# One more batch in folded form: batch 1's mirrored half goes through DRAM, and its first stage starts at unit 14

## The chip, the cores and the metric

The kernel runs on one core of one Trainium2 chip. The metric is the device time of one execution in microseconds (us). A profiled execution has a span, the time between its first and its last recorded instruction, and a device time a little longer than that. The engines are named as in the profile: PE is TensorE (matmuls) and PEld its weight loads, DVE is VectorE, ACT is ScalarE, POOL is GpSimd, SP is SyncE, which here only issues transfers.

## The reference

The input x has 8 batches of 3072 rows and 256 columns. The reference takes a Fourier transform along the rows and one along the columns, keeps the real part, and sends each of the 24576 rows through a layer with a maximum over three products:

```python
X = np.fft.fft(x, axis=1)
X = np.fft.fft(X, axis=2)
y = X.real.astype(np.float32).reshape(B * S, D)
h = np.maximum(np.maximum(y @ w1, y @ w2), y @ w3)
return (h @ w_out).astype(np.float32)
```

w1, w2, w3 are 256 x 768 and w_out is 768 x 256.

## The kernel before

**Work and units.** For each batch the transform is made in two matmul stages into a buffer `t` (`tE`, `tO`), and the layer runs on `t` in three blocks of 512 tokens with six column groups each: 18 units per batch (`UNITS`), 8 batches. By symmetry a unit makes two results at once, for the tokens and for their mirror images (`hp` and `hm`). A unit is `unit_plus` (four matmuls of 512 columns, L591 and L592), `unit_out` (a Relu on ACT, L605, a maximum on DVE, L606), `finish` of the unit before (two matmuls, L599, and again L605 and L606), and eight to ten matmuls of the output layer of the block before (L616). Beside them run `l2_even` (a product in PSUM, copied by ACT into `even`) and `l2_odd` (a product, DVE's `other` from it, L643, and POOL's `even` addition, L646). DVE adds them to the output (L670); one half of an output tile is stored by SP (L689), the other scattered by POOL (L677).

**Who runs when.** The order on each engine is the order in which the code writes instructions; there is no scheduler. The dictionary `plan` says which side work is written behind which unit: `at(b, unit, fn)` puts `fn` behind unit `unit` counted from the start of batch `b`, so unit 18 of batch 0 is unit 0 of batch 1. Each engine takes its instructions in that order, and one that waits holds all behind it. SP and POOL likewise issue their transfers in order.

**The transform of the next batch.** While batch b's units run, the transform of batch b + 1 is made (`ahead`, `begin`): seven parts s0 to s6 of stage one (`Mix.s`, L547), then six parts k0 to k5 of stage two (`Mix.k`, L571 and L573). Part s0 takes the rows d = 2 to 6 of the laid-out input, s1 7 to 11, and so on to s5 with 27 to 31; s6 takes 0, 32 and 1. A part writes one PSUM buffer of the pool `ps_f`, which has two, and ACT copies it out (L552, L555, L556; for stage two L575). Unit 0 of the next batch needs k0 and k1, unit 6 needs k2 and k3.

**The layout of the input.** Stage one needs batch b's rows in natural and in mirrored order. SP fetches a batch in four chunks of some 0.8 MB in f32 (`load_chunk`, L111 and L123) into four buffers `xs`; a chunk's buffer is used again for the next batch once all copies out of it are done.
- Batch 0 is laid out by ACT and DVE at the start and is not part of this.
- Batch 1 is unfolded. POOL copies each chunk in natural order (`turn_chunk`, L158) and in mirrored order (`reverse`, L160) into one buffer `x0`, for the last chunk in pieces (`turn_last`, L218 and L220, with `lay_last` on ACT, L209). Stage one takes two matmuls for each d, with the weights of the one and the other and the matrices `m24f` and `m24r`.
- Batches 2 to 7 are folded. `turn_part(b, ch, part)` copies a chunk on POOL: parts 0 and 1 write halves of its mirrored rows into `xb` (L178), part 1 also one row of `xw` (L182), parts 2 and 3 write halves of its natural rows into `xw` (L173). When all four chunks' mirrored halves are there, `send_turned` has SP write `xb` to DRAM in eight transfers of 96 KB with the order of partitions turned (`held`, L191). `add_turned(b, c)` then has POOL issue a transfer that reads a quarter of `held` back and adds it to `xw` in place (L199): c = 0 the rows d = 1 to 8, c = 1 9 to 16, c = 2 17 to 24, c = 3 25 to 32. After that each d takes one matmul, and only d = 0 takes two. There is one `xb`, and there are two `xw`.

For b = 0, 1 and later, the tuple `mirrored, natural, send_at, add_at` gives the units (counted from batch b) for the copies, sends and transfers of batch b + 2.

Of the kernel before, what the change touches and what calls it, by code (L numbers as in the profile page):

```python
# [33 lines left out]
def kernel(  # L34
# [9 lines left out]
    nc = tc.nc  # L44
# [101 lines left out]
                                 [xs.ap[0], [1, hi - lo], [-64, m]]))  # L146
        return done

    def turn_chunk(b, ch):

        if (b, "v") not in turned:
            x0 = x0_pool.tile([96, 68 * 128], BF16, name="x0", tag="x0")
            v = x0[:, 0:66 * 130].rearrange("p (dl bb) -> p dl bb", bb=130)
            turned[b] = (lambda d: v[:, d, 0:128], rows_back(v[:, 33:66, :]))
            turned[b, "v"] = v
        v = turned[b, "v"]
        xs = raw[b, ch]
        nc.gpsimd.tensor_copy(v[:, 0:33, ch * 32:ch * 32 + 32],  # L158
                              xs[:, 0:32 * 64].rearrange("p (bb dl) -> p dl bb", dl=64)[:, 0:33, :])
        reverse(lambda out, in_: nc.gpsimd.tensor_copy(out, in_), v[:, 33:66, :], xs,  # L160
                ch * 32, 33 if ch == 3 else 32)

    def turn_part(b, ch, part):

        xs = raw[b, ch]
# [39 lines left out]
        nc.scalar.activation(out=gw[:, 514:770], in_=gw[:, 256:512], func=AX.Copy, scale=sgn)  # L205

    def lay_last(part):
        d0, d1 = ((0, 8), (8, 16))[part]
        nc.scalar.copy(out=turned[1, "v"][:, d0:d1, 96:128],  # L209
                       in_=raw[1, 3][:, 0:32 * 64].rearrange("p (bb dl) -> p dl bb", dl=64)[:, d0:d1, :])  # L210

    def turn_last(half):

        v = turned[1, "v"]
        xs = raw[1, 3]
        d0, d1 = ((0, 17), (17, 33))[half]
        if half:
            nc.gpsimd.tensor_copy(v[:, 16:33, 96:128],  # L218
                                  xs[:, 0:32 * 64].rearrange("p (bb dl) -> p dl bb", dl=64)[:, 16:33, :])
        reverse(lambda out, in_: nc.gpsimd.tensor_copy(out, in_), v[:, 33:66, :], xs, 96, 33,  # L220
                32 + d0, 32 + d1)

    def rows_back(v):
        return lambda d: v[:, 32 - d, 0:128] if d else v[:, 32, 1:129]
# [617 lines left out]
    def fetch(b, ch):  # L842
# [1 line left out]

    ahead = (("s0",), ("s1",), ("s2",), ("s3",), ("s4",), ("s5",), ("s6",),
             ("k0",), ("k1",), ("k2",), ("k3",), ("k4",), ("k5", "end"))
    begin = {0: (11, 12, 13, 13, 14, 14, 15, 16, 16, 17, 18, 19, 20),
             1: (11, 12, 12, 13, 13, 14, 14, 15, 16, 17, 18, 19, 20),
             2: (10, 11, 11, 12, 12, 13, 13, 14, 15, 16, 17, 18, 19),
             B - 2: (8, 8, 9, 9, 10, 11, 11, 12, 13, 14, 15, 16, 17)}  # L850
# [7 lines left out]
    for (u, fn) in ((0, prep_some), (0, prep_some), (0, lambda: tab_sines(7, 10, (2,))),  # L858
                    (1, prep_some), (1, prep_some), (1, prep_some),
                    (2, lambda: m.k(2)), (2, prep_some), (2, lambda: tab_sines(10, 13, (0,))),  # L860
                    (3, prep_some), (3, lambda: tab_sines(10, 13, (1, 2))),
                    (4, lambda: m.k(3)), (4, prep_some), (5, prep_some), (5, l2_first),
                    (6, lambda: m.k(4)), (7, lambda: m.k(5)), (7, m.end),
                    (0, lambda: turn_chunk(1, 0)), (2, lambda: tab_minus(10, 13, nc.gpsimd)),
                    (2, lambda: turn_chunk(1, 1)),
                    (5, lambda: turn_chunk(1, 2)),
                    (7, lambda: turn_last(0)), (8, lambda: turn_last(1)),
                    (8, lambda: lay_last(0)), (9, lambda: lay_last(1)), (20, signed)):
        at(0, u, fn)
    for ch in range(4):  # L870
        at(0, (6, 7, 9, 11)[ch], lambda ch=ch: fetch(2, ch))
    for b in range(B - 1):
        for i, whats in enumerate(ahead):
            for what in whats:
                at(b, begin.get(b, steady)[i], lambda b=b, what=what: piece(b + 1, what))
        if b + 2 < B:
            mirrored, natural, send_at, add_at = (
                ((11, 11, 12, 13, 14, 15, 16, 17), (12, 13, 15, 16, 18, 18, 19, 20), 18, 22),
                ((5, 6, 9, 10, 11, 12, 13, 14), (7, 8, 12, 14, 15, 16, 17, 18), 15, 19),
                ((4, 5, 6, 7, 8, 9, 10, 11), (8, 10, 12, 13, 14, 15, 16, 17), 12, 18))[min(b, 2)]  # L880
            for i in range(8):
# [89 lines left out]
```

## Time and profile before

| | |
|---|---|
| median of 3 runs | 404.83 us (404.59 to 404.92) |
| the profiled execution | 404.64 us, span 402.9 us |
| PE busy | 386.0 us, 96% of the span |
| POOL busy | 292.0 us, 72% |
| DVE busy | 308.9 us, 77% |
| ACT busy | 265.5 us, 66% |
| moved by DMA | 62.06 MB, 154 GB/s |

The page gives busy times and shares per engine, then groups of instructions: line, engine, operation, output<-input, shape, count, then busy time and the mean of one in ns, then the idle time of the engine before them and what ended it. A timeline row is the start in us from the span's beginning, the time in us, and the instruction with its count; where a stretch holds several of the same kind, it runs from the first to the last. On SP and POOL the time of a transfer's row is that of issuing it, not of its data. The DMA rows of a window give the packets that moved in it, by size, and the share per queue: q1 is SP's queue, q0 that of POOL. A matmul's own duration is that of a pipeline, longer than the distance from one to the next.

### The profile page before, as it was taken

Reading aid. Unit: us, or ns where it says so; the run is one execution under the profiler, and the core shown is the slowest. Engines: PE = TensorE matmul, PEld = TensorE weight load, DVE = VectorE, ACT = ScalarE, POOL = GpSimd, SP = SyncE. Lnnn points to the kernel's source line nnn. Section 1 sums busy time; section 2 is a strip of 40 time slices with the busy share of each in tenths; the row PEclk is TensorE's granted clock in tenths of the full one; section 3 lists DMA queues with packets and bytes.
Section 4 is the critical chain, followed back from the end, with each engine's and each line's share of the span. In section 5 each row is a group of like instructions: output and inputs, shape, how many; then the busy total and the mean of one; then the engine's idle time right before and its main releaser. Section 6 shows DMA issues by size and latency. Waiting matters only on the chain.

```text
span 402.9 us, 8560 instructions
## 1 busy us (share of the span) xinstructions
PE 386.0 (96%) x2829; PEld 260.6 (65%) x2877; DVE 308.9 (77%) x556; ACT 265.5 (66%) x489; POOL 292.0 (72%) x394
## 2 busy tenths in 40 slices
PE   0999999999999999999999999999999999999996
PEld 0465667666676667666666666666677676666665
DVE  8898776788777877687776887787777877678884
ACT  6787767655866667756766677666766676655550
POOL 9599889879986998679877888768967524323521
PEclk9999999999999999999999999999999999999999
DMA  9989897789778838875478928886234411211214
GB/s 117 188 199 179 157 226 197 174 213 196 186 197 214 192 120 217 193 184 159 114 200 186 227 78 222 197 191 179 81 103 114 123 55 74 84 52 54 103 57 156
DMA packets 127597, 62.06 MB, mean 154 GB/s; under 512 B 111616, under 2 KB 116736, under 8 KB 126976
## 3 DMA queue, kind: packets, MB, share of 16 engines
q1 hardware_dynamic: 101976, 42.21, 42.3%
q0 software_dynamic: 24640, 18.98, 23.8%
q8 instruction: 22, 0.36, 0.4%
q10 hardware_dynamic: 936, 0.33, 0.3%
q14 instruction: 23, 0.19, 0.2%
HBM read 33.74 MB, written 29.88 MB: 158 GB/s over the span
## 4 chain that ended last, share of the span: by engine, by line
PE 85%; DVE 4%; DMA 3%; POOL 2%; ACT 2%; issue 2%; DVEq 0%; SPq 0%; POOLq 0%; ACTq 0%
PE po L616 29%; PE pse L591 16%; PE pse L599 14%; PE pse L592 12%; PE ps L571 3%; PE ps L573 3%; PE po L640 3%; PE pl L629 2%; PE ps L547 2%; POOL x L111 2%; DMA raw_w<-in_moe_w_dram 2%; DVE hm L606 2%; ACT stmp L605 2%; DMA x<-in_x_dram 2%; DVE other L643 1%
## 5 line engine op out<-in xcount | busy, mean ns | idle before, releaser
L605 ACT ACTIVATE stmp<-pse 128x512 bf16<-128x512 f32 x288 | 170.8, 600 | 52.6 <-PE pse L592 26.2
L606 DVE TENSOR_TENSOR hp<-pse,stmp 128x512 bf16<-128x512 f32 x144 | 99.5, 691 | 80.1 <-ACT stmp L605 51.8
L646 POOL TENSOR_TENSOR even<-even,other 128x256 f32<-128x256 f32 x92 | 70.1, 762 | 74.5 <-DVE other L643 74.2
L591 PE MATMUL pse<-t,gE 128*128 128x512 bf16 x288 | 109.1, 379 | 2.5
L606 DVE TENSOR_TENSOR hm<-pse,stmp 128x512 bf16<-128x512 f32 x144 | 99.2, 689 | 3.3 <-ACT stmp L605 3.1
L592 PE MATMUL pse<-t,gO 128*128 128x512 bf16 x249 | 94.3, 379 | 0.0
L616 PE MATMUL po<-wout_bf,hp 128*128 128x256 bf16 x576 | 85.9, 272 | 0.0
L616 PE MATMUL po<-wout_bf,hm 128*128 128x256 bf16 x570 | 85.3, 273 | 0.3
L599 PE MATMUL pse<-t,gD 128*128 128x512 bf16 x279 | 83.7, 379 | 0.1
L677 POOL DMA_INDIRECT out_dram<-ot,rows_m x53 | 53.8, 1015 | 20.2 <-DVE ot L670 10.7
L616 PEld LDWEIGHTS <-hp 128*128 128x128 bf16 x576 | 56.3, 98 | 17.3 <-issue 2.5
L616 PEld LDWEIGHTS <-hm 128*128 128x128 bf16 x576 | 56.4, 98 | 16.5
L670 DVE TENSOR_TENSOR ot<-po,even 128x512 f32<-128x512 f32 x92 | 62.8, 682 | 0.0
L173 POOL CAST xw<-xs 96x544 bf16<-96x544 f32 (+1 forms) x48 | 53.2, 1120 | 0.0
L178 POOL CAST xb<-xs 96x512 bf16<-96x512 f32 x48 | 52.4, 1100 | 0.0
L575 ACT CAST t<-ps 128x512 bf16<-128x512 f32 x48 | 27.9, 585 | 34.8 <-PE ps L573 34.7
L599 PEld LDWEIGHTS <-gD 128*128 128x128 bf16 x288 | 28.1, 98 | 32.2
L643 DVE SCALAR_TENSOR_TENSOR other<-twice,po 128x256 f32<-128x256 f32 x92 | 43.8, 476 | 0.1
L592 PEld LDWEIGHTS <-gO 128*128 128x128 bf16 x288 | 28.1, 98 | 20.4 <-issue 1.9
L591 PEld LDWEIGHTS <-gE 128*128 128x128 bf16 x288 | 28.2, 98 | 19.5 <-issue 0.7
L552 ACT CAST z_all<-ps 128x480 bf16<-128x480 f32 x46 | 24.8, 560 | 22.0 <-PE ps L547 21.9
L632 ACT COPY even<-pl 128x512 f32<-128x512 f32 x46 | 27.0, 587 | 9.7 <-PE pl L629 8.6
(178 smaller groups left out, 370.9 us busy)
## 6 DMA issues: line engine op xcount, KB each, us to landing
xs<-in_x_dram SPq DMA_DIRECT2D x84, 198.0 KB
out_dram<-ot SPq DMA_DIRECT2D x39, 256.0 KB
xs<-in_x_dram SPq DMA_DIRECT2D x28, 192.0 KB
held<-xb SPq DMA_DIRECT2D x48, 96.0 KB
xw<-held POOLq DMA_DIRECT2D x24, 192.0 KB
raw_w<-in_moe_w_dram SPq DMA_DIRECT2D x4, 384.0 KB
out_dram<-ot SPq DMA_DIRECT2D x12, 128.0 KB
x<-in_x_dram POOLq DMA_DIRECT2D x8, 120.0 KB
```

The source lines that it names most:

```text
L173: nc.gpsimd.tensor_copy(v[:, d0:d1, ch * 32:ch * 32 + 32], xs[:, 0:32 * 64].rearrange("p (bb dl) -> p dl bb", dl=64)[:, d0:d1, :])
L178: nc.gpsimd.tensor_copy(mir[:, d0:d1, c0:c0 + 32], bass.AP(xs.tensor, xs.offset + 33 * 64 - 1 - d0, [xs.ap[0], [-1, d1 - d0], [-64, 32]]))
L591: nc.tensor.matmul(pse[:, 0:n], gE[i][:, js], te, start=True, stop=False)
L592: nc.tensor.matmul(pse[:, 0:n], gO[i][:, js], to, start=False, stop=True)
L599: nc.tensor.matmul(pse, gD[i][:, js], to, start=False, stop=True, skip_group_check=True)
L605: nc.scalar.activation(out=stmp[:, 0:n], in_=pses[0][:, 0:n], func=AX.Relu)
L606: nc.vector.tensor_tensor(out=dst, in0=src3, in1=stmp[:, 0:n], op=ALU.max)
L616: nc.tensor.matmul(po, hcols(jc), wout_bf[:, jc * 256:(jc + 1) * 256], start=False, stop=(jc == NJC - 1), skip_group_check=True)
L643: nc.vector.scalar_tensor_tensor(out=other, in0=twice, scalar=po[:, 256:257], in1=po[:, 0:256], op0=ALU.mult, op1=ALU.subtract)
L646: nc.gpsimd.tensor_tensor(out=line[:, 256:512], in0=line[:, 0:256], in1=other, op=ALU.add)
L670: nc.vector.tensor_tensor(out=parts, in0=po.rearrange("p (i c) -> p i c", i=2), in1=lin.rearrange("p (i c) -> p i c", i=2), op=ALU.add)
L677: stored(nc.gpsimd.indirect_dma_start(out.rearrange("(n two) c -> n (two c)", two=2) if pair else out, bass.IndirectOffsetOnAxis(ap=rows_m ...
```

## The change

Batch 1 takes the folded form. `turn_chunk` and `turn_last` are gone. POOL makes batch 1's layout with 15 calls of `turn_part`, behind units 0 to 10 of batch 0, and ACT's `lay_last` makes the sixteenth piece (now 17 rows d in two steps, where it was 16). The eight sends stand behind unit 8, the four accumulating transfers behind units 12, 12, 13 and 13. Stage one of batch 1 stands behind units 14 to 16 in place of 11 to 15, and stage two one unit later than before, k0 and k1 both behind unit 17. Stage one of batch 1 has 32 matmuls less (34 in place of 66).

The copies of batch 2 stand one to three units later, its sends at unit 20 in place of 18, its transfers from unit 24 in place of 22; a few copies of batch 3 stand one unit later. Batch 2's third and fourth fetch stand one unit later, batch 3's first three one or two units later.

In the order of SP, batch 1's eight sends stand behind batch 2's first two chunks and one store. In the order of POOL, the four transfers stand together, ahead of batch 2's first copy and of the `even` addition of unit 14.

```diff
-    def turn_chunk(b, ch):
...
     def lay_last(part):
-        d0, d1 = ((0, 8), (8, 16))[part]
-        nc.scalar.copy(out=turned[1, "v"][:, d0:d1, 96:128],
+        d0, d1 = ((0, 8), (8, 17))[part]
+        nc.scalar.copy(out=turned[1][:, d0:d1, 96:128],
...
-    def turn_last(half):
...
-    begin = {0: (11, 12, 13, 13, 14, 14, 15, 16, 16, 17, 18, 19, 20),
+    begin = {0: (14, 14, 15, 15, 16, 16, 16, 17, 17, 18, 19, 20, 21),
...
-                    (0, lambda: turn_chunk(1, 0)), (2, lambda: tab_minus(10, 13, nc.gpsimd)),
-                    (2, lambda: turn_chunk(1, 1)),
-                    (5, lambda: turn_chunk(1, 2)),
-                    (7, lambda: turn_last(0)), (8, lambda: turn_last(1)),
+                    (2, lambda: tab_minus(10, 13, nc.gpsimd)),
                     (8, lambda: lay_last(0)), (9, lambda: lay_last(1)), (20, signed)):
         at(0, u, fn)
+    for (u, ch, part) in ((0, 0, 0), (0, 0, 1), (0, 0, 2), (0, 0, 3), (2, 1, 0), (2, 1, 1),
+                          (2, 1, 2), (4, 1, 3), (5, 2, 0), (5, 2, 1), (6, 2, 2), (7, 3, 0),
+                          (7, 3, 1), (9, 2, 3), (10, 3, 3)):
+        at(0, u, lambda ch=ch, part=part: turn_part(1, ch, part))
+    at(0, 8, lambda: send_turned(1))
+    for c in range(4):
+        at(0, 12 + c // 2, lambda c=c: add_turned(1, c))
     for ch in range(4):
-        at(0, (6, 7, 9, 11)[ch], lambda ch=ch: fetch(2, ch))
+        at(0, (6, 7, 10, 12)[ch], lambda ch=ch: fetch(2, ch))
...
             mirrored, natural, send_at, add_at = (
-                ((11, 11, 12, 13, 14, 15, 16, 17), (12, 13, 15, 16, 18, 18, 19, 20), 18, 22),
-                ((5, 6, 9, 10, 11, 12, 13, 14), (7, 8, 12, 14, 15, 16, 17, 18), 15, 19),
+                ((13, 14, 14, 15, 16, 17, 18, 19), (15, 16, 17, 18, 20, 21, 22, 23), 20, 24),
+                ((6, 7, 9, 10, 11, 12, 13, 14), (8, 9, 12, 14, 15, 16, 17, 18), 15, 19),
                 ((4, 5, 6, 7, 8, 9, 10, 11), (8, 10, 12, 13, 14, 15, 16, 17), 12, 18))[min(b, 2)]
...
-                    at(b, ((15, 18, 20, 26), (11, 15, 17, 23), (11, 14, 16, 22))[min(b, 2)][ch],
+                    at(b, ((17, 19, 22, 26), (11, 15, 17, 23), (11, 14, 16, 22))[min(b, 2)][ch],
```

More of the change, by code (lines that the diff above doesn't have):

```diff
@@ L147, in reverse @@
         return done
-    def turn_chunk(b, ch):
[L151 to L161, printed above, removed]
     def turn_part(b, ch, part):
@@ L207, in lay_last @@
     def lay_last(part):
-        d0, d1 = ((0, 8), (8, 16))[part]
-        nc.scalar.copy(out=turned[1, "v"][:, d0:d1, 96:128],
+        d0, d1 = ((0, 8), (8, 17))[part]
+        nc.scalar.copy(out=turned[1][:, d0:d1, 96:128],
                        in_=raw[1, 3][:, 0:32 * 64].rearrange("p (bb dl) -> p dl bb", dl=64)[:, d0:d1, :])
-    def turn_last(half):
[L214 to L221, printed above, removed]
     def rows_back(v):
```

## The prediction

> **What bounds the kernel now.** I read the page first, its busy shares and its chain.
>
> ```profile
> span 402.9 us, 8560 instructions
> PE 386.0 (96%) x2829; PEld 260.6 (65%) x2877; DVE 308.9 (77%) x556; ACT 265.5 (66%) x489; POOL 292.0 (72%) x394
> PE 85%; DVE 4%; DMA 3%; POOL 2%; ACT 2%; issue 2%; DVEq 0%; SPq 0%; POOLq 0%; ACTq 0%
> ```
>
> TensorE is busy for 96% of the span and is 85% of the chain. So a matmul taken away is time gained, and any time in which TensorE has to wait for its next operand is time lost; nothing later gives it back. The other engines matter only where they deliver something late. The change does both things: it takes matmuls away, and it gives one stage an operand with a longer way to go. So I read the timeline of TensorE at the place, batch 0's units 14 and 15 (columns: start, us, instruction, count).
>
> ```profile
> 58.49 0.21 PE L547 MATMUL ps<-m24f,x 96*128 96x96 bf16 x1
> ...
> 59.37 0.38 PE L591 MATMUL pse<-t,gE 128*128 128x512 bf16 x1
> ...
> 61.65 0.21 PE L547 MATMUL ps<-m24f,x 96*128 96x96 bf16 x1
> ...
> 62.50 0.81 PE L591 MATMUL pse<-t,gE 128*128 128x512 bf16 x2
> ```
>
> Unit 14 starts at 59.37, its own matmuls end at 61.65, then come two parts of stage one (20 matmuls), and unit 15 starts at 62.50. There is no gap anywhere. The 20 matmuls from 58.49 to 59.37 take 0.88 us, so one costs 0.044 us of TensorE, not the 0.2 us of its pipelined duration.
>
> **What is removed.** Unfolded, stage one of a batch has 66 matmuls (two for each of 33 rows d); folded it has 34 (row 0 has two). 32 fewer times 0.044 is 1.4 us. All of it is on the path. This is the whole possible gain.
>
> **When stage one now wants its data.** Before, four parts stood ahead of unit 14's end (after units 11, 12, 13, 13), 40 matmuls or 1.75 us. They move behind, so unit 14 ends at 61.65 - 1.75 = 59.9, and there TensorE stands before part s0, whose first weights (rows 2 to 6) lie in the piece that accumulating transfer 0 adds to. Part s1 (rows 7 to 11) needs transfer 1 as well.
>
> **When the data can be there.** It goes GpSimd copies, eight sends on SP, four accumulating transfers from GpSimd. First GpSimd, from its timeline and its groups:
>
> ```profile
> 30.52 2.04 POOL L158 CAST x<-xs 96x1056 bf16<-96x1056 f32 x1
> 46.05 1.17 POOL L220 CAST x<-xs 96x561 bf16<-96x561 f32 x1 [1.06 <-DMA xs<-in_x_dram]
> 53.83 0.72 POOL L646 TENSOR_TENSOR even<-even,other 128x256 f32<-128x256 f32 x1 [1.61 <-DVE other L643]
> L178 POOL CAST xb<-xs 96x512 bf16<-96x512 f32 x48 | 52.4, 1100 | 0.0
> L173 POOL CAST xw<-xs 96x544 bf16<-96x544 f32 x24 | 28.0, 1167 | 0.0
> L173 POOL CAST xw<-xs 96x512 bf16<-96x512 f32 x24 | 25.8, 1073 | 0.0
> L182 POOL CAST xw<-xs 96x32 bf16<-96x32 f32 x24 | 6.2, 259 | 0.0
> L199 POOL DMA_DIRECT2D xw<-held x24 | 26.8, 1178 | 0.6 <-POOL even L646 0.6
> L646 POOL TENSOR_TENSOR even<-even,other 128x256 f32<-128x256 f32 x92 | 70.1, 762 | 74.5 <-DVE other L643 74.2
> ```
>
> The first copy of batch 1 starts at 30.52. A chunk costs 2 x 1.10 + 0.26 + 1.17 + 1.07 = 4.7 us. Chunks 0 and 1 with a table operation of 1.2 us and one `even` (0.76) bring it to 41.9; chunk 2's mirrored copies, one `even` and a natural part to 46.3; chunk 3, which the second row shows landed at 46.05, is mirrored by 48.8. Behind it stand three `even`s, two scattered stores of about 1 us, two natural parts, and then a fourth `even`, that of unit 12, whose operand comes from DVE. The `even` of unit 11 ran at 53.83 after such a wait; unit 12 is 2.3 us later, so this one is done near 57. In all batch 1 now costs GpSimd 8 x 1.10 + 4 x 0.26 + 7 x 1.12 + 4 x 1.18 = 22.4 us where six copies of 2.04 and about 3.5 us for the last chunk were 15.7. These 6.7 us cost TensorE nothing by themselves, because the queue of SP is later still. SP's timeline:
>
> ```profile
> 40.88 3.03 SPq L123 DMA_DIRECT2D xs<-in_x_dram  x5
> 44.01 8.24 SPq L111 DMA_DIRECT2D xs<-in_x_dram  x8
> 52.34 1.22 SPq L689 DMA_DIRECT2D out_dram<-ot  x1
> 53.66 3.96 SPq L111 DMA_DIRECT2D xs<-in_x_dram  x4
> 74.68 4.12 SPq L191 DMA_DIRECT2D held<-xb  x8
> 199.81 4.77 SPq L191 DMA_DIRECT2D held<-xb  x8
> ```
>
> In the changed program's order the eight sends of batch 1 stand right behind batch 2's first two chunks (44.01, eight transfers) and one store (52.34). Nothing ahead of them moves, since chunk 3 of batch 1 holds SP until 43.9 either way. So the first send is issued at 53.6, five microseconds after its data was ready. How long the eight then take, from the DMA view in windows (the sends are the packets that are not under 8 KB):
>
> ```profile
> DMA packets 259, 0.88 MB, mean 147 GB/s; under 512 B 139, under 2 KB 139, under 8 KB 162
> DMA packets 2382, 1.75 MB, mean 208 GB/s; under 512 B 2126, under 2 KB 2126, under 8 KB 2286
> DMA packets 1861, 0.47 MB, mean 174 GB/s; under 512 B 1861, under 2 KB 1861, under 8 KB 1861
> q1 hardware_dynamic: 1516, 0.61, 98.3%
> ```
>
> The first row is 74.6 to 80.6: with little else about, all 96 packets have gone 5.9 us after the first issue at 74.68. The second is 199.8 to 208.2: behind a fetch the 96 took 8.4 us. The third is the first 2.7 us of that, in which five sends were issued and not one packet of theirs moved: 1861 small ones of the fetch went first. The fourth is 53.6 to 56.2 of this profile, just when the new sends will be issued: SP's queue alone keeps the engines 98.3% busy with batch 2. So it is the loaded case: 7.9 us, near the second row's end of 5.9 to 8.4, and the sends are through at 61.5 (59.5 to 62.0). GpSimd reached the first accumulating transfer at 57 and waits 4.5 us there. Queued behind that wait are the other three (1.18 us each), batch 2's copies, and the `even` of unit 14, which then runs at about 61.5 + 4.7 + 1.1 = 67.3 to 68.1; DVE's addition to the output waits for it, so this is what would be late next if the transfers were quick.
>
> What an accumulating transfer takes, from the GpSimd timeline and the DMA windows 305.8 to 307.5, 307.5 to 312.0 and 216.4 to 221.4:
>
> ```profile
> 213.39 2.07 POOL L199 DMA_DIRECT2D xw<-held  x2
> DMA packets 0, 0.00 MB, mean 0 GB/s; under 512 B 0, under 2 KB 0, under 8 KB 0
> xw<-held POOLq DMA_DIRECT2D x2, 192.0 KB
> q0 software_dynamic: 414, 0.39, 58.0%
> q0 software_dynamic: 368, 0.41, 52.2%
> ```
>
> After two are issued nothing at all moves for 1.7 us, on idle engines; then their 0.39 MB take 4.5 us. That is 6.2 us for two with nearly nothing beside them. The pair issued at 213.39 beside a fetch was through at 221.4, 8.0 us later. Batch 2's third and fourth chunk will run beside the new ones, so I take 7.7: transfers 0 and 1 are there at 61.5 + 7.7 = 69.2 (65.7 with both light ends, 70.0 with both loaded ends). Two units need transfers 2 and 3 later, and by then those are there too.
>
> **The sum.** Unit 15 starts at 69.2 in place of 62.50: +6.7 us, in which the removed matmuls of four parts are already counted. Then four folded parts follow that used to be ahead, 4 x 5 x 0.044 = +0.9, less 0.1 for the shorter part s6. Three parts now stand behind unit 16 and share two PSUM buffers, so s6 waits for the copy of s4; and k1, which used to follow unit 16, follows unit 17, with only two matmuls (0.43 us) between it and the unit that reads its copy:
>
> ```profile
> L552 ACT CAST z_all<-ps 128x480 bf16<-128x480 f32 x46 | 24.8, 560 | 22.0 <-PE ps L547 21.9
> L575 ACT CAST t<-ps 128x512 bf16<-128x512 f32 x48 | 27.9, 585 | 34.8 <-PE ps L573 34.7
> ```
>
> A copy of 0.56 less the 0.22 of s5, plus about 0.2 to get there: +0.5 (0 to 1). A copy of 0.585 and a matmul's 0.27 less 0.43: +0.4 (0 to 1). Last the clock. TensorE's own rows at the kernel's start, after 10 us of idling (windows, the `warm` matmuls alone):
>
> ```profile
> 10.00:13.90 3.90, 3.89 (x10) 1.00 2.65 124
> 13.90:16.20 2.30, 2.30 (x12) 1.00 1.88 133
> ```
>
> Ten matmuls of 512 columns fill the first 3.9 us, twelve the next 2.3: about half speed at first (the column of the granted clock says 1.00 in both, so the pace must be read from the counts). A wait of 69.2 - 59.9 = 9 us, broken by one short part, is nearest to these 10 us, so I count one such start: 3.9 us at half speed, +1.9 (0 to 3.9, if it is paid twice). The Trainium skill, "TensorE: Matmul & The Clock Gate", Part 1, has the clock halved after one idle window of about 3.4 us and restored after one busy window; by it the price is due even at the short end of my range of waits, and without it the sum would be 413.0.
>
> Batch 2's copies and transfers go two units later, about 4.6 us. Before, its last transfer was issued at 93.67, and its parts s3 and s4 stood at 105.64 to 106.5:
>
> ```profile
> 93.67 1.61 POOL L199 DMA_DIRECT2D xw<-held  x1
> 105.64 0.83 PE L547 MATMUL ps<-m24f,xw 96*128 96x96 bf16 x10
> ```
>
> Issued at 98.3 and taking 7 to 8 us there, it ends at 105 to 106, just in time for s4. I take 0, with up to 2 us lost, since batch 0's delay gives GpSimd time. Batch 3's few copies a unit later cost 0: its transfers keep their unit. ScalarE's second laying copy grows by one row in eight, which its idle time hides.
>
> Together 6.7 + 0.9 - 0.1 + 0.5 + 0.4 + 1.9 = +10.3 us on the profiled execution's 404.64, which is 0.2 below the median of 404.83: 415.0.
>
> **Rivals.** *Shorter wait, clock kept.* Sends at 59.5 and light transfers put unit 15 at 65.7, +3.2, and with +0.8 for the parts and little else it is 409 to 412.5. For it: GpSimd's transfers have a queue of their own beside SP's. Against: the 98.3%.
>
> *The wait spreads.* GpSimd's 4.5 us of standing, and the transfers beside two more chunks, make transfers 2 and 3 late for s3 and s4 too, batch 2 pays its 2 us, the clock is paid twice: 10.3 + 2 + 2 + 2 is 418 to 421. The late `even` above speaks for it; that the stalled TensorE gives everything else time speaks against.
>
> *The fold pays (the other side).* If transfers 0 and 1 are through when unit 14 ends, only -1.4 + 0.5 + 0.4 or less stays, 403.4 to 404.3. It turns on one number: the sends must be through by 59.9 - 6.2 = 53.7, but that is when the first is issued. Only if batch 2's fetch ran much faster, or the sends did not queue behind it, could this be; the window with five issues and no packet speaks against.
>
> *It changes nothing.* A wait of just 1.4 us less the small terms, 404 to 405.6, needs the same luck in part.
>
> **How the numbers follow.** Forecast (412.5 to 418) 0.50, shorter wait 0.27, spread 0.15, the fold pays 0.05, nothing 0.03. The likeliest gives 415.0. The range from 408.5 to 421.0 leaves out the two cases on the fast side (0.08) and the far end of the spread. A change of 0.2% (0.8 us) is about what can be told from none: slower 0.93, within it 0.02, faster 0.05.
>
> **What will show it.** In the profile after: a wait of TensorE's weight load at stage one (L547) of some 6 to 8 us near 60, released by a DMA, and a second shorter one at s1; the sends on SP at 53.6; GpSimd idle from 57 to 61 and four transfers in a row; TensorE's first unit after it slow; from batch 2 on the same pace as before. A stage one of batch 1 without a gap, or sends that leave earlier, would prove me wrong; so would a unit at full pace right after the wait, for the clock term.

## The result, and the profile after

The changed kernel takes 419.45 us (median; 417.93 to 421.13) where the kernel before took 404.81 us beside it (404.1 to 405.64). The ratio is 1.036, with a 95% interval of 1.035 to 1.038: 14.6 us slower. The profiled execution took 419.37 us with a span of 417.6 us, beside 404.64 us before, a difference of 14.73 us.

The page of the changed kernel, its busy times, its granted clock in 40 slices and its chain:

```profile
span 417.6 us, 8571 instructions
PE 391.0 (94%) x2845; PEld 260.1 (62%) x2845; DVE 309.2 (74%) x556; ACT 266.1 (64%) x489; POOL 297.5 (71%) x407
PEclk9999995899999999999999999999999999999999
PE 83%; DMA 5%; POOL 5%; ACT 2%; SPq 2%; DVE 1%; issue 1%; ACTq 0%; POOLq 0%
```

TensorE has fewer weight loads than before (2845 for 2877) and is nevertheless "busy" 5 us longer. Most of that is not time: the trace of the kernel before lacks the records of 48 of its 2877 matmuls, this one lacks none, and a run below with the same matmuls as the kernel before, all recorded, is busy for 389.5 us (batches 2 and 3 later). The rest goes with the third line: in two of the 40 slices, from about 63 to 83 us, the clock that the throttle granted is 0.5 and 0.8. And in the chain, DMA, POOL and SP's queue have grown, from 3%, 2% and 0% to 5%, 5% and 2%. The slow clock points to one place. The groups of waits (engine, tile and line; what it waited for; us in total, times, longest) and TensorE's timeline show it. (Line numbers of the changed kernel are 25 lower than before: stage one is L522, the units' first matmul L566.)

```profile
PE ps L522 <- DMA xw<-held: 11.7, 2, 10.2
POOL xw L185 <- DMA xs<-in_x_dram: 5.7, 2, 5.4
```

```profile
58.22 0.38 PE L566 MATMUL pse<-t,gE 128*128 128x512 bf16 x1
...
70.89 0.72 PE L522 MATMUL ps<-m24f,xw 96*128 96x96 bf16 x7 [10.22 <-DMA xw<-held]
73.10 0.42 PE L522 MATMUL ps<-m24f,xw 96*128 96x96 bf16 x3 [1.49 <-DMA xw<-held]
73.32 0.63 PE L566 MATMUL pse<-t,gE 128*128 128x512 bf16 x1
...
77.78 0.38 PE L566 MATMUL pse<-t,gE 128*128 128x512 bf16 x1
...
81.09 0.18 PE L522 MATMUL ps<-m0f,xw 96*128 96x52 bf16 x1 [0.20 <-ACT z_all L527]
...
85.25 0.38 PE L566 MATMUL pse<-t,gE 128*128 128x512 bf16 x1 [0.29 <-ACT t L550]
```

Unit 14 starts at 58.22; at its end TensorE stands 10.22 us before s0, which needs accumulating transfer 0, and 1.49 us before s1, which needs transfer 1. Unit 15 starts at 73.32 where it was 62.50, and its matmul takes 0.63 us instead of 0.38. The two last rows are the small waits of s6 and of batch 1's unit 0 (85.25). What delivered so late is read on SP and on POOL, where a transfer's row is its issuing:

```profile
44.33 7.36 SPq L111 DMA_DIRECT2D xs<-in_x_dram  x8
51.79 1.02 SPq L664 DMA_DIRECT2D out_dram<-ot  x1
52.91 4.13 SPq L177 DMA_DIRECT2D held<-xb  x8
57.14 5.82 SPq L111 DMA_DIRECT2D xs<-in_x_dram  x4
```

```profile
46.80 2.10 POOL L164 CAST xb<-xs 96x512 bf16<-96x512 f32 x2 [0.71 <-DMA xs<-in_x_dram]
...
62.67 3.99 POOL L185 DMA_DIRECT2D xw<-held  x4 [5.39 <-DMA xs<-in_x_dram]
```

The mirrored data is complete at 48.9, when POOL's last two copies of it end. The sends wait behind batch 2's fetch in SP's queue until 52.91. GpSimd stands from 57.3 to 62.67 for them. (The row puts its 5.39 us down to a transfer of `in_x`. But the instruction that waits reads `held`, and GpSimd's wait for the eight transfers into `held` ends at 61.7.) Then the first two transfers, which TensorE needs, take until 73.1: 10.4 us from the first issue.

Where the 14.73 us lie, by the starts of units in the two profiled executions. 0.5 us is at the start: unit 0 of batch 0 stands at 24.70 instead of 24.18, ahead of all that is discussed here, and in the runs below it lay anywhere between 23.3 and 24.95.

| step | before | after | lost, us |
|---|---|---|---|
| unit 15 starts, less the 0.5 of the start | 62.50 | 73.32 | 10.3 |
| unit 15 to unit 16 | 2.58 | 4.46 | 1.9 |
| unit 16 to unit 17 | 3.18 | 3.42 | 0.2 |
| unit 17 to batch 1's unit 0 | 3.15 | 4.05 | 0.9 |
| batch 1's unit 0 to batch 2's unit 0 | 46.20 | 47.09 | 0.9 |

Of the last 0.9, 0.43 is the part k2, which now stands behind that boundary instead of ahead of it; the rest is a short wait in batch 2's stage one. From batch 2 on the distance is 14.73 to the end.

### The profile page after: what moved, and what is told of

It reads as the page before. It is cut to its first block, busy times and chain, and to the rows that moved or that the text cites. A ratio compares the mean times of both kernels' runs of the same rounds, so it can differ in the third digit from the quotient of the medians.

```text
span 417.6 us, 8571 instructions
## 1 busy us (share of the span) xinstructions
PE 391.0 (94%) x2845; PEld 260.1 (62%) x2845; DVE 309.2 (74%) x556; ACT 266.1 (64%) x489; POOL 297.5 (71%) x407
## 4 chain that ended last, share of the span: by engine, by line
PE 83%; DMA 5%; POOL 5%; ACT 2%; SPq 2%; DVE 1%; issue 1%; ACTq 0%; POOLq 0%
PE po L591 27%; PE pse L566 14%; PE pse L574 14%; PE pse L567 14%; PE ps L522 3%; POOL x L111 3%; PE ps L546 2%; PE ps L548 2%; PE po L615 2%; DMA xw<-held 2%; PE pl L604 2%; DMA xs<-in_x_dram 2%; SPq L111 1%; DMA x<-in_x_dram 1%; DVE hm L581 1%
## 5 line engine op out<-in xcount | busy, mean ns | idle before, releaser
L621 POOL TENSOR_TENSOR even<-even,other 128x256 f32<-128x256 f32 x92 | 71.8, 780 | 78.2 <-DVE other L618 77.8
L566 PE MATMUL pse<-t,gE 128*128 128x512 bf16 x288 | 109.6, 381 | 0.8 <-ACT t L550 0.3
L567 PE MATMUL pse<-t,gO 128*128 128x512 bf16 x288 | 109.5, 380 | 0.0
L574 PE MATMUL pse<-t,gD 128*128 128x512 bf16 x288 | 86.1, 381 | 0.0
L652 POOL DMA_INDIRECT out_dram<-ot,rows_m x53 | 53.9, 1017 | 19.5 <-DVE ot L645 11.7
L164 POOL CAST xb<-xs 96x512 bf16<-96x512 f32 x56 | 63.6, 1143 | 1.7 <-DMA xs<-in_x_dram 1.7
L159 POOL CAST xw<-xs 96x512 bf16<-96x512 f32 (+1 forms) x55 | 60.9, 1119 | 0.0
L566 PEld LDWEIGHTS <-gE 128*128 128x128 bf16 x288 | 28.3, 98 | 19.7 <-issue 0.9
L185 POOL DMA_DIRECT2D xw<-held x28 | 30.7, 1230 | 6.2 <-DMA xs<-in_x_dram 5.7
```

The lines of the kernel that those rows point to most:

```text
L159: nc.gpsimd.tensor_copy(v[:, d0:d1, ch * 32:ch * 32 + 32], xs[:, 0:32 * 64].rearrange("p (bb dl) -> p dl bb", dl=64)[:, d0:d1, :])
L164: nc.gpsimd.tensor_copy(mir[:, d0:d1, c0:c0 + 32], bass.AP(xs.tensor, xs.offset + 33 * 64 - 1 - d0, [xs.ap[0], [-1, d1 - d0], [-64, 32]]))
L566: nc.tensor.matmul(pse[:, 0:n], gE[i][:, js], te, start=True, stop=False)
L567: nc.tensor.matmul(pse[:, 0:n], gO[i][:, js], to, start=False, stop=True)
L574: nc.tensor.matmul(pse, gD[i][:, js], to, start=False, stop=True, skip_group_check=True)
L621: nc.gpsimd.tensor_tensor(out=line[:, 256:512], in0=line[:, 0:256], in1=other, op=ALU.add)
```

## The experiments

Three theories go with the changed kernel. **A**: the order of SP's queue makes the sends late, and all the rest follows. **B**: the way through DRAM is too long wherever the sends stand. **C**: the fold itself does not pay. The letters of later ones stand with them.

**The sends ahead of the fetch.** Batch 2's fetches are written two units or one later, so that the eight sends come first on SP.

```diff
-        at(0, (6, 7, 10, 12)[ch], lambda ch=ch: fetch(2, ch))
+        at(0, (8, 9, 11, 13)[ch], lambda ch=ch: fetch(2, ch))
```

> Theory A (the sends of batch 1 stand behind batch 2's first two chunks in SP's order, and so TensorE waits for its operand): with the sends ahead of that fetch they start at about 49, when their data is ready, and are through by 55; GpSimd reaches the transfers at 57 without a wait, TensorE's unit 15 starts at 65 to 68 in place of 73.3, and the time falls by 5 to 8 us to 411 to 414. Rival B (the DMA engines are full, the order does not matter): sends and transfers share the same 16 engines with the same bytes, unit 15 stays within 2 us of 73.3 and the time within 2 us of 419.4. Rival C (GpSimd has too much work): its copies are unchanged, the transfers are issued at 62 as before, no change.

It took 416.24 us (ratio 1.030, 1.025 to 1.035). SP, POOL and TensorE in this run:

```profile
48.02 5.08 SPq L177 DMA_DIRECT2D held<-xb  x8
53.14 11.84 SPq L111 DMA_DIRECT2D xs<-in_x_dram  x8
```

```profile
57.37 3.99 POOL L185 DMA_DIRECT2D xw<-held  x4 [0.34 <-issue]
...
71.98 1.06 POOL L164 CAST xb<-xs 96x512 bf16<-96x512 f32 x1 [6.36 <-DMA xs<-in_x_dram]
```

```profile
63.83 0.72 PE L522 MATMUL ps<-m24f,xw 96*128 96x96 bf16 x7 [3.43 <-DMA xw<-held]
65.37 0.42 PE L522 MATMUL ps<-m24f,xw 96*128 96x96 bf16 x3 [0.81 <-DMA xw<-held]
65.59 0.63 PE L566 MATMUL pse<-t,gE 128*128 128x512 bf16 x1
...
70.70 0.38 PE L566 MATMUL pse<-t,gE 128*128 128x512 bf16 x1
...
114.56 0.50 PE L522 MATMUL ps<-m24f,xw 96*128 96x96 bf16 x8 [0.44 <-DMA xw<-held]
116.16 0.26 PE L522 MATMUL ps<-m24f,xw 96*128 96x96 bf16 x2 [1.11 <-DMA xw<-held]
```

The sends leave at 48.02, GpSimd does not stand any more, and unit 15 starts at 65.59 instead of 73.32. So the order on SP is worth 7.7 us at this place, as A said. Yet only 3.2 us reach the end by the medians, 4.8 us in this execution (414.59 beside 419.37). Unit 15 at half clock takes 5.1 us (65.59 to 70.70) where it took 4.46, and the fetch that was pushed back takes its share at batch 2: the last two rows of TensorE are batch 2's stage one, now waiting for its own transfers, and units 12 and 13 of batch 1 take 2.8 us longer than in the kernel before, 2.3 us longer than in the changed kernel. GpSimd's second row is one of batch 2's copies. It stands for 6.36 us until a chunk of the late fetch has landed; batch 1's sends had landed long before, near 55.6.

**No accumulating transfers for batch 1.** All else of the change stays.

```diff
-    for c in range(4):
-        at(0, 12 + c // 2, lambda c=c: add_turned(1, c))
```

> Leaves out batch 1's four accumulating transfers, so batch 1's transform lacks its mirrored half; all else stays. Theory A: the wait of TensorE behind unit 14 is gone entirely and with it the slow clock after it; what is left is 1.4 us gained, 1.2 us lost to s6 and k1 behind their copies, and about 0.5 in batch 2: 404.5 to 405.5. Rival C (GpSimd's copies are late, or its longer queue holds up the layer's additions): the natural copies and the additions stand in the same order, so a wait of several us stays and the time is 408 or more.

It took 406.13 us (ratio 1.0033, 1.0013 to 1.0053), a little over what was expected. With nothing to wait for before s0, 13.3 of the 14.6 us are gone, the slow clock with them. What is left is at batch 2: s4 there waits, and the unit around it takes 3.85 us where it took 2.95.

```profile
107.93 0.26 PE L522 MATMUL ps<-m24f,xw 96*128 96x96 bf16 x2 [0.73 <-DMA xw<-held]
```

**TensorE kept warm in the wait.** 45 matmuls of 512 columns into a buffer that nobody reads, behind unit 14.

```diff
+    def keep_busy():
+        spare = ps_f.tile([128, 512], FP32, name="spare", tag="ps")
+        for _ in range(45):
+            nc.tensor.matmul(spare, gE[0][:, 0:128], mixes[0].tE[:, 0:512], start=True, stop=True)
+
+    at(0, 14, keep_busy)
```

> As the changed kernel, with 45 matmuls of 512 columns into a spare PSUM buffer behind unit 14, 9.6 us of work that is not used, while TensorE waits there anyway. If the half-speed unit 15 comes from the idle wait: unit 15 takes 2.4 us in place of 4.0, and the time falls by 1.3 to 2 us to 417.5 to 418. If unit 15 is slow for another cause (its operands, PSUM, ACT), or the extra work delays s0: no gain, 419 to 421.

It took 415.97 us (ratio 1.027, 1.024 to 1.031), 3.5 us less than the changed kernel. The windows (from:to, us, then busy us and count of PE, PEld, DVE, ACT and POOL, the granted clock, DMA share, GB/s) around the wait and the unit after it, first of the changed kernel:

```profile
60.00:70.70 10.70, 0.67 (x7) 0.35 (x4) 1.82 (x4) 0.10 (x1) 7.83 (x10) 0.64 0.93 167
70.70:73.10 2.40, 0.72 (x8) 0.54 (x8) 0.00 (x0) 0.56 (x1) 1.21 (x3) 0.50 1.08 194
73.10:77.50 4.40, 4.40 (x23) 2.44 (x24) 1.77 (x3) 1.75 (x3) 0.01 (x1) 0.59 0.86 196
77.50:81.00 3.50, 3.32 (x36) 2.29 (x34) 1.67 (x3) 3.12 (x7) 3.50 (x5) 1.00 0.16 56
```

Then of the run with the extra matmuls:

```profile
67.40:70.50 3.10, 3.10 (x20) 1.45 (x18) 0.00 (x0) 0.00 (x0) 2.91 (x6) 1.00 1.06 185
70.50:73.50 3.00, 3.00 (x35) 2.17 (x33) 1.21 (x3) 2.01 (x4) 0.63 (x1) 1.00 0.98 230
```

The clock column falls to 0.50 in the wait and is still 0.59 through unit 15; with TensorE kept busy it is 1.00 throughout, and unit 15 takes 2.81 us (70.75 to 73.56) instead of 4.46. That is 1.65 us for the clock, as expected. The rest of the gain, 1.9 us, is why the total came below the 417.5 to 418 that were expected, and it is the data's: GpSimd issues its first transfer at 61.83, and parts s0 and s1 run from 70.32 without a wait, at most 8.7 us later, where it was 10.4. Nothing in the edit explains that. With the same fetch beside them the transfers are not equally long in every execution, and why is left open.

**Batches 2 and 3 later, batch 1 as before.** The kernel before, with only the later units of batches 2 and 3, their fetches among them, taken over from the change. Theory A with the price of zero for these units stands against a rival D, that they cost TensorE something by themselves.

```diff
-        at(0, (6, 7, 9, 11)[ch], lambda ch=ch: fetch(2, ch))
+        at(0, (6, 7, 10, 12)[ch], lambda ch=ch: fetch(2, ch))
...
-                ((11, 11, 12, 13, 14, 15, 16, 17), (12, 13, 15, 16, 18, 18, 19, 20), 18, 22),
-                ((5, 6, 9, 10, 11, 12, 13, 14), (7, 8, 12, 14, 15, 16, 17, 18), 15, 19),
+                ((13, 14, 14, 15, 16, 17, 18, 19), (15, 16, 17, 18, 20, 21, 22, 23), 20, 24),
+                ((6, 7, 9, 10, 11, 12, 13, 14), (8, 9, 12, 14, 15, 16, 17, 18), 15, 19),
...
-                    at(b, ((15, 18, 20, 26), (11, 15, 17, 23), (11, 14, 16, 22))[min(b, 2)][ch],
+                    at(b, ((17, 19, 22, 26), (11, 15, 17, 23), (11, 14, 16, 22))[min(b, 2)][ch],
```

> The kernel before with only the second part of the change: the copies, sends and transfers of batches 2 and 3 at the later units, and the fetches as changed; batch 1 unfolded as before. Theory A: this part costs 0 to 1 us, the last transfers of batch 2 just in time for s4: 404.8 to 405.8. Rival D (the later units of batches 2 and 3 carry a good part of the loss): 407 or more.

It took 406.8 us (before beside it 404.6; ratio 1.0047, 1.0031 to 1.0064), 2.2 us more and between the two expectations. TensorE's timeline in this run has two waits that the kernel before does not have:

```profile
103.39 0.27 PE L640 MATMUL po<-gw,t 128*128 128x257 bf16 x1 [0.77 <-DVE ot L670]
...
108.78 0.26 PE L547 MATMUL ps<-m24f,xw 96*128 96x96 bf16 x2 [0.86 <-DMA xw<-held]
```

The transfers of batch 2 stand closer to their use: the last is issued at 102.16 where it was 93.67, and one part waits 0.86 us for it. DVE's addition to the output makes TensorE wait 0.77 us more. In the changed kernel itself, whose batch 0 takes longer, the unit with the later of these waits is only 0.45 us longer than before (3.40 for 2.95), and there is no wait of the first kind.

**The later fetches behind the transfers.**

```diff
-        at(0, (6, 7, 10, 12)[ch], lambda ch=ch: fetch(2, ch))
+        at(0, (6, 7, 15, 16)[ch], lambda ch=ch: fetch(2, ch))
```

> As the changed kernel, with batch 2's third and fourth chunk fetched behind units 15 and 16, so that in SP's order they stand behind the next stores and do not run beside the four transfers. Theory E (the transfers were slower than forecast, 10.4 us from the issue of the first to the data of the second, because of this fetch): the sends are through near 61 as before, but transfers 0 and 1 take 6 to 7.5 us, and TensorE's unit 15 starts at 69 to 70.5 in place of 73.3. What batch 2 loses by its later chunks comes on top, 1 to 4 us at its stage one, so the total says little: 416 to 420. Rival F (four transfers issued together hold each other up, or adding in place is slow in itself): 9.5 to 11 us again, unit 15 at 72.5 to 74.

It took 419.11 us (ratio 1.036, 1.032 to 1.039) and missed its aim. What stands ahead of the third fetch on SP is only stores of blocks that were finished long before, so SP came to that fetch at 60.92 all the same, and it ran beside the transfers as ever. They took 9.5 us (60.14 to 69.65). So the run does not separate E from F. Unit 15 does start at 69.92, as E said, but for another reason: the whole execution is early (its unit 0 stands at 23.32 instead of 24.70), and the transfers were issued at 60.14 instead of 62.67. One thing it does show: the fetch began only after the first two transfers were issued, so it need not be in the queue before them for them to take that long.

**Half of batch 2's fetch left out.** The same question put in another way: E, the fetch beside the transfers makes them slow, or F, they are that slow by themselves.

```diff
+    def again(ch):
+        raw[2, ch] = raw[2, ch - 2]
+
     for ch in range(4):
-        at(0, (6, 7, 10, 12)[ch], lambda ch=ch: fetch(2, ch))
+        at(0, (6, 7, 10, 12)[ch], lambda ch=ch: fetch(2, ch) if ch < 2 else again(ch))
```

> As the changed kernel, but batch 2's third and fourth chunk aren't fetched; its copies read its first two chunks twice (batch 2's transform is of other data). So 1.6 MB less are on the way while the four transfers run, and nothing else is delayed. Theory E (the transfers were slow because of that fetch): transfers 0 and 1 have their data 6 to 7.5 us after the issue of the first, and unit 15 starts at 68.5 to 70; the time falls by 3.5 to 6 us to 413.5 to 416. Rival F (four together, or adding in place, are slow in themselves): 9.5 to 11 us again, unit 15 at 72 to 74, 418 to 420.

It took 415.94 us (ratio 1.027, 1.024 to 1.030), and unit 15 starts at 70.17. The rows of GpSimd and TensorE:

```profile
63.38 3.99 POOL L185 DMA_DIRECT2D xw<-held  x4 [6.62 <-DMA out_dram<-ot]
```

```profile
69.95 0.42 PE L522 MATMUL ps<-m24f,xw 96*128 96x96 bf16 x3 [0.93 <-DMA xw<-held]
```

The share per queue while transfers 0 and 1 move their data (packets, MB, share of 16 engines), in the changed kernel from 66.0 to 73.1 and here from 65.6 to 69.9:

```profile
q0 software_dynamic: 639, 0.71, 70.9%
q1 hardware_dynamic: 1403, 0.52, 30.9%
```

```profile
q0 software_dynamic: 498, 0.52, 78.7%
```

In the changed kernel SP's queue (q1) has nearly a third of the engines beside GpSimd's (q0), and without the fetch it moves nothing. In the 2.7 us before that, 63.3 to 66.0, when GpSimd's transfers had just been issued, it had most of them:

```profile
q1 hardware_dynamic: 1348, 0.39, 78.2%
q0 software_dynamic: 117, 0.04, 17.5%
```

That earlier stretch costs little: without the fetch, too, GpSimd's queue moves only 0.02 MB from 63.3 to 65.6, on engines that are otherwise idle. The difference is in the stretch in which the data moves, 4.3 us here and 7.1 us there.

Without the fetch the two transfers take 6.5 us from the first issue (63.38 to 69.9) instead of 10.4, with four in a row as before. F, which expected 9.5 to 11, falls, and E holds: the fetch beside them makes them longer. By how much is known less well. These are two executions that differ by 3.9 us, but with the same fetch beside them the run with the extra matmuls had its data within 8.7 us, so it is some 2 to 4 us. And 6.5 us remain when no other queue moves anything.

**No transfers, and batches 2 and 3 where they were.** Theory G: the fold gains its 1.4 us if its data waits for nothing, and GpSimd's longer copying is free. The edit takes away the transfers of batch 1 and puts back the units of batch 1's two stages and nearly all those of batches 2 and 3 (batch 2's last two fetches stay one unit later, other than the expectation says).

```diff
-    begin = {0: (14, 14, 15, 15, 16, 16, 16, 17, 17, 18, 19, 20, 21),
+    begin = {0: (11, 12, 13, 13, 14, 14, 15, 16, 16, 17, 18, 19, 20),
...
-    for c in range(4):
-        at(0, 12 + c // 2, lambda c=c: add_turned(1, c))
...
-                ((13, 14, 14, 15, 16, 17, 18, 19), (15, 16, 17, 18, 20, 21, 22, 23), 20, 24),
-                ((6, 7, 9, 10, 11, 12, 13, 14), (8, 9, 12, 14, 15, 16, 17, 18), 15, 19),
+                ((11, 11, 12, 13, 14, 15, 16, 17), (12, 13, 15, 16, 18, 18, 19, 20), 18, 22),
+                ((5, 6, 9, 10, 11, 12, 13, 14), (7, 8, 12, 14, 15, 16, 17, 18), 15, 19),
...
-                    at(b, ((17, 19, 22, 26), (11, 15, 17, 23), (11, 14, 16, 22))[min(b, 2)][ch],
+                    at(b, ((15, 18, 20, 26), (11, 15, 17, 23), (11, 14, 16, 22))[min(b, 2)][ch],
```

> Leaves out batch 1's four accumulating transfers (its transform lacks its mirrored half), and puts stage one and stage two of batch 1 and all copies, sends, transfers and fetches of batches 2 and 3 back to the units of the kernel before. What folding saves on TensorE, with nothing late: by the count of matmuls 32 x 0.044 = 1.4 us, 403.0 to 403.6. If the longer work of GpSimd (6.7 us more in batch 0, 1.2 of it for the transfers left out here) makes batch 2 late all the same: 404 to 405.5, with a wait at batch 2's stage one.

It took 406.35 us (before beside it 404.88; ratio 1.0039, 1.0011 to 1.0067): no gain, and for a reason that none of the theories had. POOL, DVE and TensorE in this run:

```profile
60.87 2.07 POOL L164 CAST xb<-xs 96x512 bf16<-96x512 f32 x2 [5.40 <-DMA xs<-in_x_dram]
63.08 0.72 POOL L621 TENSOR_TENSOR even<-even,other 128x256 f32<-128x256 f32 x1
```

```profile
63.83 0.69 DVE L645 TENSOR_TENSOR ot<-po,even 128x512 f32<-128x512 f32 x1 [2.49 <-POOL even L621]
```

```profile
64.57 0.27 PE L615 MATMUL po<-gw,t 128*128 128x257 bf16 x1 [2.07 <-DVE ot L645]
...
66.06 0.63 PE L566 MATMUL pse<-t,gE 128*128 128x512 bf16 x1
```

There is one `xb`. POOL's first mirrored copy of batch 2 writes it, and may not before batch 1's sends have read it; those landed at 60.67, and the copy starts at 60.87. (Again the row names a transfer of `in_x`.) Behind the copy stands an `even` addition, behind that DVE's addition to the output, behind that TensorE. The clock adds to it: after the wait of 2.07 us unit 16 begins at half pace (0.63 us for a matmul) and takes 4.57 us instead of 3.18. The later units that the change gives to batch 2 hide just this: in the run without transfers above, GpSimd's first copy of batch 2 waits in the same way, until 61.95, but TensorE does not wait for it, and its unit 15 takes 2.81 us where it takes 5.01 here.

**The same without the sends.** One more line is taken away.

```diff
-    at(0, 8, lambda: send_turned(1))
```

> Leaves out batch 1's sends as well as its accumulating transfers (its transform lacks its mirrored half); stage one and two of batch 1 and all work for batches 2 and 3 at the units of the kernel before. Theory G (the 1.4 us are there, and what took them in the last run was GpSimd's first copy for batch 2, which waited for the sends to have read the one xb buffer, with an addition for the layer behind it): without sends nothing waits, and the time is 403.2 to 403.8. Rival C (GpSimd's longer copying alone eats the gain): 404.5 or more, with a wait of TensorE near units 14 to 16 all the same.

It took 403.40 us (before beside it 404.55; ratio 0.9976, 0.9962 to 0.9989): 1.15 us faster. The page:

```profile
PE 385.0 (96%) x2797; PEld 259.0 (64%) x2845; DVE 308.7 (77%) x556; ACT 265.6 (66%) x489; POOL 294.1 (73%) x403
```

TensorE's busy time falls by 1.0 us (each of the two traces lacks 48 matmuls). The profiled execution is a slow one of its kind, 404.40 us, but the gain shows at its place: from unit 5 of batch 0 to batch 1's unit 0 it takes 34.49 us (36.67 to 71.16) where the kernel before takes 35.62 (35.79 to 71.41), 1.13 us less. GpSimd's first mirrored copy of batch 2 runs at 56.69 without a wait, though its chunk was fetched no earlier than in the last run (issued from 45.30 on, there from 43.80 on), so it was the sends that held it there. So the fold pays, G, and C falls; and all of POOL's extra copying is in this run and costs nothing. This run, without sends and transfers, is not a working version. One that has them can hardly gain more than these 1.15 us.

**The sends from ScalarE.** The fetches keep the places that the change gives them, and the sends still leave early. H is the rival that the give-back after the early sends had nothing to do with the fetch's place.

```diff
-    def send_turned(b):
+    def send_turned(b, eng=nc.sync):
...
-            nc.sync.dma_start(out=hd[7 - i].rearrange("(a r) -> a r", a=12),
+            eng.dma_start(out=hd[7 - i].rearrange("(a r) -> a r", a=12),
...
-    at(0, 8, lambda: send_turned(1))
+    at(0, 9, lambda: send_turned(1, nc.scalar))
```

> Against the changed kernel only one thing differs: batch 1's eight sends are issued by ScalarE behind unit 9, in place of SyncE behind unit 8; all fetches keep the places that the changed kernel gives them. ScalarE comes there at about 51 and issuing costs it some 0.5 us each. Theory A (SyncE's order made the sends late; in the run with the sends ahead of the fetch 3 us were given back because batch 2's fetch came later): the sends are through at 57 to 59, transfers 0 and 1 at 65 to 67, unit 15 starts at 65 to 67 in place of 73.3, batch 2's stage one does not wait more than in the changed kernel, and the time is 411 to 414, up to 3 us more if ScalarE's issuing holds up units 9 and 10. Rival H (the give-back was not from the fetch's place but from everything after unit 15 being crowded): unit 15 as early, but batch 2's units 13 and 14 wait as in that run, and the time is 415 to 417. Rival B (the transfers of data, not the order of issuing, made the sends late): sends through at 61 or later, unit 15 at 71 or later, 417 or more.

It took 420.63 us (ratio 1.038, 1.035 to 1.041), more than any of the theories that let the sends leave early gave. ScalarE and TensorE in this run:

```profile
49.16 5.96 ACTq L177 DMA_DIRECT2D held<-xb  x8
55.22 1.08 ACT L580 ACTIVATE stmp<-pse 128x512 bf16<-128x512 f32 x2 [6.25 <-DMA held<-xb]
```

```profile
56.36 0.39 PE L566 MATMUL pse<-t,gE 128*128 128x512 bf16 x1 [5.07 <-ACT stmp L580]
...
71.14 0.72 PE L522 MATMUL ps<-m24f,xw 96*128 96x96 bf16 x7 [3.62 <-DMA xw<-held]
73.37 0.42 PE L522 MATMUL ps<-m24f,xw 96*128 96x96 bf16 x3 [1.52 <-DMA xw<-held]
```

The sends are through by 60, as A said (of their 96 packets all but one had gone by 58), and the wait before s0 is 3.62 us instead of 10.22. But ScalarE issues for 6 us, its next Relu stands behind that for 6.25 us, and TensorE 5.07 us behind the Relu: units 10 and 11 take 7.53 and 4.04 us where they took 2.28 each, 7.0 us more, most of the second at half clock. GpSimd's `even` of unit 12 comes later with them:

```profile
64.52 3.99 POOL L185 DMA_DIRECT2D xw<-held  x4 [0.31 <-issue]
```

So the transfers are issued at 64.52, take 8.8 us, and unit 15 starts at 73.59, not at the 65 to 67 that A expected. What is saved before s0 is lost at units 10 and 11. The time 411 to 414 was missed because the price of issuing on ScalarE was put at 0 to 3 us and was 7.0.

As unit 15 is no earlier than in the changed kernel, this run cannot settle H: all that follows had as much time as there. Two other rows speak against H. In the run without transfers unit 15 starts at 61.52, earlier than in any other run with the change's later units, with the fetch in its place, and units 12 and 13 of batch 1 take 6.7 us where they took 8.5 with the early sends (but batch 1's four transfers are missing there). And with the early sends GpSimd stood 6.36 us for the late fetch itself.

Nor do A or B hold alone. The run with early sends moved unit 15 by 7.7 us, so order counts, against B; but even there TensorE still waited 3.43 and 0.81 us, and with the fetch away 6.5 us are the transfers' own. With early sends unit 14 ended at 60.4, so transfers of 6.5 us would have to be issued by 53.9, and GpSimd came to them at 57.37. A version that beats the kernel before would need the sends early on an engine with nothing else to do, the transfers earlier in GpSimd's order, a second `xb`, and the fetch elsewhere; this was not tried, and it would have about 1.15 us to gain.

## Why the prediction was right, and where not

The forecast was slower, 415.0 us with a range to 421.0. The measured 419.45 lies in the range, 4.4 us above the likeliest value, in the region of the rival that let the wait spread; that rival's mechanism, however, is not what happened, since after the first two transfers no part of batch 1 waited for a third or a fourth.

- **The gain of 1.4 us.** Right in kind; 1.15 us in the run that has only the fold.
- **Unit 14's end.** Forecast 59.9; it was near 60.7, of which 0.5 is this execution's late start.
- **The sends.** Issued at 53.6 by the forecast, from 52.91 to 57.04 in the trace; through at 61.5 by the forecast, near 61.7 in the trace. The loaded case, taken from the window in which five sends moved no packet, was the right one.
- **GpSimd's stop.** Reached at 57 and 4.5 us long by the forecast; 57.3 and 5.4 us. The first transfer was issued at 62.67, not when the sends were through; for that step, about 1 us, the sum had nothing.
- **Transfers 0 and 1: this is the term that was mis-sized.** "So I take 7.7", between 6.2 on idle engines and 8.0 beside a fetch. It was 10.4 us. The 8.0 came from one pair beside one fetch and was taken for the loaded end; with a fetch beside them the runs here have 7.9, at most 8.7, 8.8, 9.5 and 10.4, so the loaded end was too short, and the changed kernel's profiled execution lies at the far end of it. The light end was right: 6.5 us with the later fetch left out. Four transfers issued in a row are not the cause, since that run has them too; what sets the place between 7.9 and 10.4 is open. Of unit 15's 10.3 us, 6.7 were forecast. Of the other 3.6 us, 2.7 are this term, 0.7 the later first issue (62.67 for 61.5, less the 0.5 of the start), and 0.2 part s1.
- **The clock.** Forecast +1.9; 1.65 by the run that kept TensorE warm. Paid once. The trace after shows what the page before could only show by counts, 0.50 from 63.02 on and 0.59 in the unit behind the wait. The Trainium skill, "TensorE: Matmul & The Clock Gate", Part 1, on which that step leant beside its row, has the clock halved after an idle window of about 3.4 us and restored after at least one busy window. The traces agree in kind: a wait of 3.43 us was enough in the run of the early sends, and full pace came back 3.6 us after TensorE took up steady work in the changed kernel (73.10 to 76.67) and 4.9 us there (65.37 to 70.25). But a wait of 2.07 us was enough too, in the run without transfers whose batches stood where they were.
- **The parts behind.** The steps after unit 15 were forecast at 3.6 us together (1.9 + 0.9 - 0.1 + 0.5 + 0.4). The table above has 3.0 to batch 1's unit 0, and 0.43 more for k2 behind it: 3.4.
- **Batch 2's later units.** "I take 0, with up to 2 us lost": about 0.45 in the changed kernel, and 2.2 us where batch 0 has no delay to give. There the last transfer was issued at 102.16, not 98.3.
- **GpSimd's 6.7 us more copying at nothing.** Right, as the fold alone shows. What the prediction did not name is the one `xb`: the sends hold up GpSimd's copies of the next batch, and that is what batch 2's later units hide. The order of the instructions does not show it, since it is a buffer's reuse and no wait for data.

That the result lies inside the range owes something to the range's breadth: the likeliest value was 4.4 us too low, and the chance given to 412.5 to 418 was 0.50. With 10.4 in place of 7.7 and 0.45 in place of 0 the forecast's own sum is 415.0 + 2.7 + 0.45 = 418.2, and with the start's 0.5 it is 418.7, beside the profiled 419.37.

## What to carry to other kernels

A matmul saved is worth its 0.044 us only if the operand's longer way ends before TensorE comes to it: add up that way from the last producer, queue by queue, before counting the saving, and here 1.15 us stood against a loss of 13.3. A small transfer that something waits for belongs ahead of a bulk prefetch in its queue (here that moved its reader by 7.7 us), but what is pushed back must then be followed to its own reader, one batch later. A shared staging buffer is a hidden order between two batches: ask who may write it next, and what stands behind that writer.

## What the runs showed of the hardware

Before s0 TensorE idled 3.43 us in the run with early sends, and that halved the clock as fully as the 10 us of the changed kernel did:

```profile
60.20:63.50 3.30, 0.20 (x2) 0.00 (x0) 1.35 (x3) 0.00 (x0) 3.11 (x5) 0.99 0.92 151
63.50:65.40 1.90, 0.75 (x8) 0.57 (x9) 0.00 (x0) 0.56 (x1) 1.90 (x4) 0.50 1.12 199
65.50:70.60 5.10, 5.10 (x27) 2.85 (x26) 1.78 (x3) 1.75 (x3) 0.12 (x1) 0.53 0.96 243
```

The granted clock is 0.99 through the idle stretch, 0.50 in the next 1.9 us, and 0.53 through 5.1 us of full work. What the slow clock costs does not go by the length of the wait: unit 15 took 4.46 us after a wait of 10.22, and 5.05, 5.29 and 5.11 us after 8.32 (later fetches behind the transfers), 8.16 (half of the fetch left out) and 3.43.

The stretches at 0.50 are whole numbers of one step. They last 13.65 us in the changed kernel (63.02 to 76.67), 6.82 us with early sends (63.43 to 70.25) and 3.42 us in the run without transfers whose batches stood where they were (65.46 to 68.88): four, two and one times 3.41. There the wait was only 2.07 us, and in the 3.41 us ahead of the stretch TensorE was busy for 1.34. So a gap shorter than the step, with work on both sides of it, can halve the clock; how much work would have kept it up, these runs do not show.

The time of accumulating transfers was less steady than anything else: the first two took 6.5 us with half the fetch left out, and 7.9, at most 8.7, 8.8, 9.5 and 10.4 us in runs in which a fetch of batch 2 ran beside them. The six runs of the changed kernel spread over 3.2 us; the kernel before spreads over 1.4 to 2.6 us, from one set of its runs to the next.
